# Two head pairs per attention step with merged products, and the rounded parts of q and k and the sums' 1e-9 on GpSimd

## The chip, the cores and the metric

The kernel runs on one core of one Trainium2 chip. The metric is the device time of one execution in microseconds (us); lower is better. The engines are named as in the profile: PE is TensorE's products, PEld its loads of fixed operands, DVE is VectorE, ACT is ScalarE, POOL is GpSimd, SP is SyncE, which issues most DMAs.

## The reference

```python
def _attn_ref(q, k, v, n_global, n_local):        # 4 batches, 8 heads, 768 tokens, 64 wide
    scores = scale * np.matmul(q, k.transpose(0, 1, 3, 2)) + bias     # a slope per head times the distance
    scores = np.where(is_global | is_local, scores, -1000000000.0)     # 8 first keys, 96 last keys
    a = np.exp(scores - np.max(scores, axis=-1, keepdims=True))
    a = a / (np.sum(a, axis=-1, keepdims=True) + 1e-09)
    return np.matmul(a, v)

def reference(...):
    x = attention, its heads side by side           # [3072, 512]
    x = _moe_ref(x, w_gate, w1, w2)                 # each token to the best of 8 experts, 512 -> 1024 -> 512, times its gate
    return _moe2_ref(x, w_in, w_out, a, b)          # rational feed-forward, 512 -> 2048 -> 512
```

## The kernel before, in words

Attention comes first and takes the first quarter of the time. It has 24 units (u: a batch and a tile of 128 queries), each of four head pairs (hp). Since only 96 local and 8 global keys count, a unit's window is 232 keys wide (WIN), or 128 for a tile that starts a sequence. A loop over t (L746 on) goes through the 96 steps (u, hp). Everything is emitted in the order of that loop, and each engine works through its own instructions in that order. A step t has five groups of products on PE, each for another pair:

- stD (L644) of step t-5: the attended values, transposed back and multiplied with the gate's weights, into ps_ox (L647); DVE scales them into x (L653) and lw (L657)
- stA (L575) of step t: the scores, 6 products on half the rows, `sj` (L586), as a rounded part and a rest of q and k (qh, ql and two parts in kr)
- stC (L630) of step t-3: the probabilities times v, into ps_o (L638), copied to oT by ACT (L641)
- stB (L608) of step t-1: 4 transposes of probabilities into pt (L616), copied to pT (L624; of one pair in four on ACT, L622)
- emit_tstep (L503): 2 of the 4 transposes of the next tile of q or k, ps_qk (L512).

After each second half of a tstep ACT copies ps_qk to `raw` and rounds that to qh or a part of kr (L524), and POOL subtracts the two for the rest (L525). Between A and B, stA2 (L589) has DVE add the mask and find the extreme of a row (`nn`, `mn`, L600) and ACT take the exponential with the sum `sm` (`pp`, L604). In stB DVE adds 1e-9 to the sums (L619) and inverts them (L626).

Between such instructions `fill()` emits one small step of routing each, mostly on DVE: which expert a token goes to, its gate, its sorted position `pos` (L215), and then scatters on POOL (`scatter`, L136, tid) and a table (L198). Tokens are routed in groups of 4, 7, 6, 3, 3 and 1 units. Once the fourth group is routed, the first tokens of expert 0 are fetched early: their numbers are read back (L128, eidx) behind all scatters, their rows gathered (L250, raw), and, in the string TAILS that emits what follows the loop, scaled on DVE (letter G, `scale_x`, L254) and transposed (X), and the expert is begun (E). TAILS also drains the last steps (B, C, D with the distance from the end), and F is a fill. POOL also splits the first expert's weights during attention (wa_l, L315). Scores have three PSUM banks (psS), pt two, ps_qk, ps_o and ps_ox one each.

Of the kernel before, what the change touches and what calls it, by code (L numbers as in the profile page):

```python
# [20 lines left out]
P = 128  # L21
# [12 lines left out]
TAILS = "D5 G F1 C3 C2 B1 X0 C1 F3 D4 X1 D3 F3 F7 F1 E2 D2 F2 F1 E2 F2 F2 F1 F3 E1 F5 D1"  # L34
# [5 lines left out]
WARM2 = 2, 2, 2, 4  # L40
LOADS = ("k0", "ll", "lg", "q0", "k1", "q1")
POOLQ = ""
MS = (7, 2, 4, 2)
# [5 lines left out]
def kernel(  # L49
# [206 lines left out]
    def put_xT(xh, xl, x, t, r, ps=None):  # L256
        """Puts a token tile of r rows, transposed, in columns t*P on of both parts."""
# [13 lines left out]
    def early_steps(w, x, h, banks, ends=(0, FC1 + KC)):  # L271
        """The early tile's products in small steps, each followed by what it leaves to do for other engines."""
# [44 lines left out]
    def expert_chunks(wh, wl, e1, e2):  # L317
        """Split steps of an expert's weights; e1: [DM, F1] and e2: [F1, DM] sources."""
# [10 lines left out]
    # ================= attention, window of the fast path =================  # L329
    with first as sx:  # L330
# [8 lines left out]
        # the inputs' rings lie where the first expert's operands will  # L339
# [61 lines left out]
        # masks: distance times slope, plus NEG where nothing is kept; the first for the tiles that start a  # L401
        # sequence, the second for the others, whose window is the local tail, the global keys and the tile
# [33 lines left out]
        # constants that are not needed at once  # L436
# [40 lines left out]
        # q and k transposed, [d of two heads, pair, token], in two float32r parts. The keys of a sequence lie  # L477
        # side by side, each tile behind a copy of the global keys, so that a window is one stretch of columns.
# [6 lines left out]
        def emit_first(nm, part):  # L485
            """A half of the first tile's heads, without detours."""
# [16 lines left out]
        def emit_tstep(step, part):  # L503
# [9 lines left out]
            if part == 1:  # L513
# [10 lines left out]
                nc.scalar.activation(qh, raw, AF.Copy)  # L524
# [19 lines left out]
        seq = [(u, hp) for u in range(units) for hp in range(NP)]  # L544
# [12 lines left out]
        # the second mask's own tile is the first mask, but for the columns of the global keys  # L557
# [4 lines left out]
        def fill(pe=False):  # L562
            """One small step of the routing, between two large ones; those with products only where pe."""
# [11 lines left out]
        def stA(u, hp):  # L575
            bb, i = divmod(u, NI)
            w = P if i == 0 else WIN
            s2 = []
            k1 = (i + 1) * GK
            for j in range(2):  # L580
                sj = psS.tile([P, 512], F32, name="sj")
                s2.append(sj)
            for n, (x, y) in enumerate(((0, 0), (0, 1), (1, 0))):
                for j in range(2):
                    hd = slice(j * D, (j + 1) * D)
                    nc.tensor.matmul(s2[j][:, 0:w], qT[u][x][hd, hp, :], kr[hd, y, hp, k1 - w:k1], start=n == 0, stop=n == 2)  # L586
            st[u, hp] = s2

        def stA2(u, hp):  # L589
            i = u % NI  # L590
            w = P if i == 0 else WIN
            s2 = st[u, hp]
            sm = wk.tile([P, 2], F32, name="sm", bufs=5)
            pr = []
            for j in range(2):
                h = 2 * hp + j
                nn = wk.tile([P, WIN], F32, name=f"nn{j}")
                mn = wk.tile([P, 1], F32, name=f"mn{j}")
                bmh = bm[:, h, WIN:WB] if i == 0 else bm[:, h, 0:WIN]
                nc.vector.tensor_tensor_reduce(nn[:, 0:w], s2[j][:, 0:w], bmh, op0=ALU.add, op1=ALU.min,  # L600
                                               scale=1.0, scalar=3.0e38, accum_out=mn)
                fill()
                pp = wk.tile([P, WIN], F32, name=f"pp{j}")
                nc.scalar.activation(pp[:, 0:w], nn[:, 0:w], AF.Exp, scale=-1.0, bias=mn, accum_out=sm[:, j:j + 1])  # L604
                pr.append(pp)
            st[u, hp] = [pr, sm]

        def stB(u, hp):  # L608
            i = u % NI
            w2 = P // 2 if i == 0 else HWIN  # L610
            pr, sm = st[u, hp]
            pt = psT.tile([P, 2, 2, P], F32, name="pt")
            for j in range(2):
                pv = pr[j][:, 0:2 * w2].rearrange("p (c r) -> p r c", r=2)
                for r in range(2):
                    nc.tensor.transpose(pt[0:w2, j, r, :], pv[:, r, :], ident)  # L616
            pT = wk.tile([HWIN, 2, 2, P], F32, name="pT", bufs=3)
            rs = wk.tile([P, 2], F32, name="rs", bufs=7)
            nc.vector.tensor_scalar(rs, sm, 1e-9, None, op0=ALU.add)  # L619
            fill()  # L620
            if hp in ONACT:
                nc.scalar.activation(pT[0:w2], pt[0:w2], AF.Copy)  # L622
            else:
                nc.vector.tensor_copy(pT[0:w2], pt[0:w2])  # L624
            fill()
            nc.vector.reciprocal(rs, rs)  # L626
            fill()
            st[u, hp] = [pT, rs]

        def stC(u, hp):  # L630
            i = u % NI
            w2 = P // 2 if i == 0 else HWIN
            pT, rs = st[u, hp]
            vt = vts[u]
            ox = psM.tile([P, 512], F32, name="ps_o")
            for r in range(2):
                for j in range(2):
                    nc.tensor.matmul(ox[j * D:(j + 1) * D, 0:P], vt[0:w2, 2 * hp + j, r, :], pT[0:w2, j, r, :],  # L638
                                     start=(r == 0), stop=(r == 1))
            oT = wk.tile([P, P], F32, name="oT", bufs=4)  # L640
            nc.scalar.activation(oT, ox[:, 0:P], AF.Copy)  # L641
            st[u, hp] = [oT, rs]

        def stD(u, hp):  # L644
            oT, rs = st.pop((u, hp))
            ox = psM.tile([P, 512], F32, name="ps_ox")
            nc.tensor.matmul(ox[:, 0:P + 2 * E], oT, iw[:, hp, :], start=True, stop=True)  # L647
            if hp == 0:
# [4 lines left out]
            nc.vector.tensor_tensor(x[:, hp * P:(hp + 1) * P].rearrange("p (j d) -> p j d", j=2),  # L653
                                    ox[:, 0:P].rearrange("p (j d) -> p j d", j=2),
                                    rs.unsqueeze(2).to_broadcast([P, 2, D]), op=ALU.mult)
            fill()
            nc.vector.tensor_tensor(lw[:, 2 * hp:2 * hp + 2, :],  # L657
                                    ox[:, P:P + 2 * E].rearrange("p (j e) -> p j e", j=2),
                                    rs.unsqueeze(2).to_broadcast([P, 2, E]), op=ALU.mult)
            if hp == NP - 1:  # L660
# [15 lines left out]
        # the first tokens of expert 0, from when all but the last groups are routed; done again below if too few  # L676
# [21 lines left out]
        def e_step(n, lag=1):  # L698
            """n small steps of the early tile; what they leave to other engines comes some steps later."""
# [46 lines left out]
        for t in range(L):  # L746
            if t < L:
                u, hp = seq[t]
                bb, i = divmod(u, NI)
                if 0 < t < 3:  # L750
                    emit_tstep(*nxt.pop(0))
                if t == NP + 2:
                    filler.append(look)
                if hp == (u == 0):
                    if u + 2 < units:
                        load_v(u + 2)
                    for lb, li in loads.get(u, []):
                        load_qk(lb, li)
                if hp == 0 and u >= 5 and u % 2 == 1 and wst:
                    dh, dl, src, n = wst.pop(0)  # L760
                    wld.append((dh, dl, load_w(src, n)))
                if hp == 0 and 2 <= u < 2 + sum(groups[-2:]):
                    r0 = (units - sum(groups[-2:]) + u - 2) * P
                    nc.sync.dma_start(xs[r0:r0 + P, :], zrow)
# [903 lines left out]
```

## Time and profile before

| what | value |
|---|---|
| time, median of 3 runs | 1171.92 us (1169.7 to 1175.31) |
| span of the profiled execution | 1169.0 us |
| PE busy | 1109.0 us (95%) |
| DVE, ACT, POOL busy | 954.6 us (82%), 760.1 us (65%), 434.6 us (37%) |

The span is that of one execution under the profiler, from first to last instruction; it is 2.9 us below the median of the runs and inside their spread to 0.7 us. Start times below are microseconds from the start of the span. The page's shares are means over stages with different limits; attention is the stretch from about 9 to 275 us.

### The profile page before, as it was taken

The page shows a single profiled execution, that of the slowest core. Times are in us where ns is not written, and L with a number is a line of the kernel's source. Part 1 is how long each engine was busy: PE and PEld are TensorE (multiplying, and loading weights), DVE is VectorE, ACT ScalarE, POOL GpSimd, SP SyncE. Part 2 cuts the span into 40 slices and gives each one's busy share as a digit, 9 for nine tenths or more (in the row PEclk, how much of TensorE's full clock was granted, in tenths as well). Part 3 has the DMA queues.
Part 4 walks back from the last instruction along what each step waited for, and adds up shares of the span by engine and source line. Part 5 has one row for each costly group of instructions (what it writes and reads, how often), then busy time and mean ns, then how long its engine had stood idle before and what let it go on. Part 6 is the DMA issues. An engine that isn't in the chain of part 4 may idle for free.

```text
span 1169.0 us, 19466 instructions
## 1 busy us (share of the span) xinstructions
PE 1109.0 (95%) x6636; PEld 982.8 (84%) x6636; DVE 954.6 (82%) x2200; ACT 760.1 (65%) x1695; POOL 434.6 (37%) x454
## 2 busy tenths in 40 slices
PE   8998988987699999999997999999999999999997
PEld 7876776766699888999996888999999999999996
DVE  7897878774667967887667999989898998989985
ACT  5886777662254555554555777777777777777774
POOL 4253444532422323132114535344342535344342
PEclk9998989798799999999999999999999999999999
DMA  9887787403477877887663000000100000000000
GB/s 177 186 132 162 164 94 173 87 20 105 114 226 251 302 243 248 283 302 269 211 204 123 1 27 28 28 28 1 46 10 28 28 27 28 19 27 10 1 28 27
DMA packets 122820, 130.65 MB, mean 112 GB/s; under 512 B 62799, under 2 KB 92671, under 8 KB 122704
## 3 DMA queue, kind: packets, MB, share of 16 engines
q1 hardware_dynamic: 108416, 99.78, 32.7%
q0 software_dynamic: 8624, 22.48, 5.6%
q10 hardware_dynamic: 5664, 6.98, 1.6%
q8 instruction: 56, 0.92, 0.4%
q14 instruction: 60, 0.49, 0.2%
HBM read 99.60 MB, written 29.61 MB: 111 GB/s over the span
## 4 chain that ended last, share of the span: by engine, by line
PE 59%; DVE 7%; ACT 2%; issue 2%; DMA 2%; POOL 1%; ACTq 0%; POOLq 0%; DVEq 0%; SPq 0%
PE acc L268 10%; PE acc L267 10%; PE acc L269 10%; PE ph L267 7%; PE ph L268 7%; PE ph L269 7%; PE ps_t L267 3%; PE ps_t L269 3%; PE ps_t L268 3%; DVE ta L1546 1%; DVE tcc L1545 1%; DVE ta L1595 1%; PE ps_t L260 1%; DVE tcc L1605 1%; DMA ysT<-y 1%
## 5 line engine op out<-in xcount | busy, mean ns | idle before, releaser
L1560 POOL TENSOR_TENSOR gl<-tcc,gh 128x384 fp32r<-128x384 f32 x127 | 128.9, 1015 | 293.8 <-ACT gh L1554 229.1
L267 PE MATMUL acc<-wa_h,gh 128*128 128x512 f32 x384 | 150.2, 391 | 5.9 <-ACT gh L1554 4.3
L269 PE MATMUL acc<-wa_h,gl 128*128 128x512 f32 x384 | 151.4, 394 | 1.7 <-POOL gl L1560 1.7
L268 PE MATMUL acc<-wa_l,gh 128*128 128x512 f32 x384 | 151.3, 394 | 0.0
L1545 DVE SCALAR_TENSOR_TENSOR tcc<-tcc,cf,tb 128x384 f32<-128x384 f32 x128 | 117.9, 921 | 13.7 <-DVE tcc L1605 0.5
L1596 ACT ACTIVATE tb<-ta,cf 128x384 f32<-128x384 f32 x128 | 79.0, 617 | 42.8 <-DVE ta L1595 32.8
L1595 DVE SCALAR_TENSOR_TENSOR ta<-ta,cf,tb 128x384 f32<-128x384 f32 x128 | 81.4, 636 | 31.0 <-ACT tb L1590 29.7
L604 ACT ACTIVATE pp<-nn,mn 128x232 f32<-128x232 f32 (+1 forms) x192 | 88.8, 465 | 26.6 <-DVE mn L600 23.5
L1546 DVE SCALAR_TENSOR_TENSOR ta<-ta,cf,tb 128x384 f32<-128x384 f32 x128 | 103.3, 807 | 0.0
L269 PEld LDWEIGHTS acc<-wa_h,gl 128*128 128x128 f32 x384 | 72.1, 188 | 20.0 <-POOL gl L1560 4.7
L267 PE MATMUL ph<-xh,wb_h 128*128 128x384 f32 (+3 forms) x252 | 86.8, 344 | 1.7 <-DVE tcc L1605 1.2
L267 PEld LDWEIGHTS acc<-wa_h,gh 128*128 128x128 f32 x384 | 72.1, 188 | 19.0 <-ACT gh L1554 5.7
L268 PE MATMUL ph<-xl,wb_h 128*128 128x384 f32 (+3 forms) x252 | 86.3, 343 | 0.3 <-DVE xl L953 0.2
L269 PE MATMUL ph<-xh,wb_l 128*128 128x384 f32 (+3 forms) x252 | 86.1, 342 | 0.0
L268 PEld LDWEIGHTS acc<-wa_l,gh 128*128 128x128 f32 x384 | 72.0, 188 | 11.4
L616 PE MATMUL pt<-ident,pp 128*116 128x128 f32 (+1 forms) x384 | 71.6, 311 | 2.3 <-ACT pp L604 2.3
L1589 ACT ACTIVATE ta<-ph 128x384 f32<-128x384 f32 x78 | 38.1, 488 | 54.0 <-PE ph L269 54.0
L600 DVE CUSTOM_DVE_ANT_0 nn<-sj,bm 128x232 f32<-128x232 f32 (+1 forms) x192 | 65.8, 373 | 6.8 <-PE sj L586 4.7
L1551 DVE SCALAR_TENSOR_TENSOR tcc<-ta,tcc 128x384 f32<-128x384 f32 x128 | 70.4, 550 | 0.0
L616 PEld LDWEIGHTS pt<-ident,pp 128*116 128x116 f32 (+1 forms) x384 | 49.3, 185 | 20.9 <-issue 15.3
L1554 ACT ACTIVATE gh<-tcc 128x384 fp32r<-128x384 f32 x128 | 65.1, 509 | 2.3 <-DVE tcc L1551 2.3
L1601 ACT ACTIVATE tb<-tb 128x384 f32<-128x384 f32 x128 | 65.1, 509 | 0.0
(335 smaller groups left out, 3352.9 us busy)
## 6 DMA issues: line engine op xcount, KB each, us to landing
wst<-in_moe_w_dram SPq DMA_DIRECT2D x72, 512.0 KB
wst<-in_moe_w_in_dram SPq DMA_DIRECT2D x16, 512.0 KB
wst<-in_moe_w_out_dram SPq DMA_DIRECT2D x16, 512.0 KB
xs<-x SPq DMA_DIRECT2D x24, 256.0 KB
hh<-in_v_dram SPq DMA_DIRECT2D x17, 256.0 KB
wf_in<-cv POOLq DMA_DIRECT2D x16, 256.0 KB
wf_out<-cv POOLq DMA_DIRECT2D x16, 256.0 KB
wst<-wf_in SPq DMA_DIRECT2D x8, 512.0 KB
```

The source lines that it names most:

```text
L267: nc.tensor.matmul(ps, lh, rh, start=first, stop=False)
L268: nc.tensor.matmul(ps, lh, rl, start=False, stop=False)
L269: nc.tensor.matmul(ps, ll, rh, start=False, stop=last)
L600: nc.vector.tensor_tensor_reduce(nn[:, 0:w], s2[j][:, 0:w], bmh, op0=ALU.add, op1=ALU.min, scale=1.0, scalar=3.0e38, accum_out=mn)
L604: nc.scalar.activation(pp[:, 0:w], nn[:, 0:w], AF.Exp, scale=-1.0, bias=mn, accum_out=sm[:, j:j + 1])
L616: nc.tensor.transpose(pt[0:w2, j, r, :], pv[:, r, :], ident)
L1545: nc.vector.scalar_tensor_tensor(pc_, pc_, na0, pb_, op0=ALU.add, op1=ALU.mult)
L1546: nc.vector.scalar_tensor_tensor(pa_, pa_, one, pb_, op0=ALU.add, op1=ALU.mult)
L1551: nc.vector.scalar_tensor_tensor(pc_, pa_, -2.0, pc_, op0=ALU.add, op1=ALU.mult)
L1560: eng.tensor_tensor(gl, prev[2], gh.bitcast(F32), op=ALU.subtract)
L1595: nc.vector.scalar_tensor_tensor(ta, ta, b1, tb, op0=ALU.mult, op1=ALU.add)
L1596: nc.scalar.activation(tb, ta, AF.Ln, bias=one)
```

## The change

Attention's loop now takes two head pairs (HG = 2) at a time: 48 steps (u, hg), here called double steps. Each of the five groups on PE holds the products of both pairs, one behind the other: 12 for the scores in two banks (a pair at columns 0 and 256 of each), 8 for ps_o, 2 for ps_ox, 8 transposes of probabilities, and two tsteps. The copy to oT, x and lw take both pairs in one instruction. The lags are 1, 2 and 3 double steps in place of 1, 3 and 5 steps. The rounding at L524 is on GpSimd, ahead of the subtraction there, and so is the addition of 1e-9 (now L617, four columns at once); the inversion stays on DVE and stands in stC, behind the copy to oT (L651). A double step has 11 fills where two steps had 14. The lists of warm-up products and TAILS have new numbers. The diff, without the hunks that only take comments away:

```diff
-TAILS = "D5 G F1 C3 C2 B1 X0 C1 F3 D4 X1 D3 F3 F7 F1 E2 D2 F2 F1 E2 F2 F2 F1 F3 E1 F5 D1"
+TAILS = "D3 G F1 C2 B1 X0 C1 F3 D2 X1 F3 F7 F1 E2 D1 F2 F1 E2 F2 F2 F1 F3 E1 F5"
-WARM2 = 2, 2, 2, 4
+WARM2 = 4, 6
-MS = (7, 2, 4, 2)
+MS = (7, 2, 4, 4)
...
-                nc.scalar.activation(qh, raw, AF.Copy)
+                nc.gpsimd.tensor_copy(qh, raw)
                 (nc.vector if u < SUBV else nc.gpsimd).tensor_tensor(ql, raw, qh.bitcast(F32), op=ALU.subtract)
...
+        HG = 2
+        NG2 = NP // HG
+        seq = [(u, hg) for u in range(units) for hg in range(NG2)]
...
+        def stA(u, hg):
+            s2 = [psS.tile([P, 512], F32, name="sj") for j in range(2)]
+            for a in range(HG):
+                hp = HG * hg + a
+                for n, (x, y) in enumerate(((0, 0), (0, 1), (1, 0))):
+                    for j in range(2):
+                        hd = slice(j * D, (j + 1) * D)
+                        nc.tensor.matmul(s2[j][:, a * 256:a * 256 + w], qT[u][x][hd, hp, :], kr[hd, y, hp, k1 - w:k1],
+                                         start=n == 0, stop=n == 2)
...
+        def stB(u, hg):
+            rs = wk.tile([P, HG, 2], F32, name="rs", bufs=5)
+            nc.gpsimd.tensor_scalar(rs, sm, 1e-9, None, op0=ALU.add)
+            pts = []
+            for a in range(HG):
+                pt = psT.tile([P, 2, 2, P], F32, name="pt")
...
+            for a in range(HG):
+                pT = wk.tile([HWIN, 2, 2, P], F32, name="pT", bufs=3)
+                fill()
+                if HG * hg + a in ONACT:
+                    nc.scalar.activation(pT[0:w2], pts[a][0:w2], AF.Copy)
+                else:
+                    nc.vector.tensor_copy(pT[0:w2], pts[a][0:w2])
...
+        def stC(u, hg):
+            for a in range(HG):
+                for r in range(2):
+                    for j in range(2):
+                        nc.tensor.matmul(ox[j * D:(j + 1) * D, a * P:(a + 1) * P], vt[0:w2, 2 * (HG * hg + a) + j, r, :],
+                                         pTs[a][0:w2, j, r, :], start=(r == 0), stop=(r == 1))
+            oT = wk.tile([P, HG, P], F32, name="oT", bufs=2)
+            nc.scalar.activation(oT, ox[:, 0:HG * P].rearrange("p (a q) -> p a q", a=HG), AF.Copy)
+            nc.vector.reciprocal(rs, rs)
...
+            if t >= 3:
+                stD(*seq[t - 3])
+            stA(u, hg)
+            if t >= 2:
+                stC(*seq[t - 2])
+            stA2(u, hg)
...
+            if t >= 1:
+                stB(*seq[t - 1])
+            for _ in range(3 if t == 0 else 2):
+                if nxt:
+                    emit_tstep(*nxt.pop(0))
...
             fill(True)
+            fill(True)
```

First, PE's stream in the loop, one whole step of before and the start of the next (ps_ox is the output of D, sj the scores of A, ps_o that of C, pt of B, ps_qk of the transposes):

```order
L647 MATMUL ps_ox<-iw,oT 128x144
L586 MATMUL sj<-kr,qh 128x232 x4
L586 MATMUL sj<-kr,ql 128x232 x2
L638 MATMUL ps_o<-pT,hl 64x128 x4
L616 MATMUL pt<-ident,pp_1990 116x128 x2
L616 MATMUL pt<-ident,pp_1995 116x128 x2
L512 MATMUL ps_qk<-ident,xh 128x128 x2
L647 MATMUL ps_ox<-iw,oT 128x144
```

And one whole double step of the changed kernel:

```order
L659 MATMUL ps_ox<-iw,oT 128x144 x2
L588 MATMUL sj<-kr,qh 128x232 x4
L588 MATMUL sj<-kr,ql 128x232 x2
L588 MATMUL sj<-kr,qh 128x232 x4
L588 MATMUL sj<-kr,ql 128x232 x2
L647 MATMUL ps_o<-pT,hh 64x128 x8
L624 MATMUL pt<-ident,pp_1917 116x128 x2
L624 MATMUL pt<-ident,pp_1927 116x128 x2
L624 MATMUL pt<-ident,pp_1922 116x128 x2
L624 MATMUL pt<-ident,pp_1932 116x128 x2
L512 MATMUL ps_qk<-ident,xl 128x128 x4
```

The same products now stand in half as many groups, five per two pairs in place of ten.

Second, POOL's stream at a place in the middle of the loop, before, where a weight split (wa_l) stands between subtractions:

```order
L525 TENSOR_TENSOR kr<-raw,kr 128x4x128
L315 TENSOR_TENSOR wa_l<-wst,wa_h 128x1024
L525 TENSOR_TENSOR ql<-raw,qh 128x512
L525 TENSOR_TENSOR kr<-raw,kr 128x4x128
L525 TENSOR_TENSOR ql<-raw,qh 128x512
```

And a like place of the changed kernel:

```order
L315 TENSOR_TENSOR wa_l<-wst,wa_h 128x1024
L617 TENSOR_SCALAR rs<-sm 128x4
L524 CAST kr<-raw 128x4x128
L525 TENSOR_TENSOR kr<-raw,kr 128x4x128
L617 TENSOR_SCALAR rs<-sm 128x4
L524 CAST qh<-raw 128x512
L525 TENSOR_TENSOR ql<-raw,qh 128x512
```

A cast stands ahead of each subtraction, and the sums' addition (rs), which DVE's inversion reads, is queued behind subtractions and weight splits.

Third, DVE's stream at the end of attention, from the fourth group's positions (pos, L215) to the scaling of the early gathered rows (raw, L254), which stands in TAILS. Before, there are eight steps of pairs between the two (each with an x at L653); the two ends:

```order
L215 TENSOR_TENSOR pos<-em_4509,rank 128x3
L527 CAST kr<-kr 128x8x8
L653 TENSOR_TENSOR x<-ps_ox,rs 128x128
L657 TENSOR_TENSOR lw<-ps_ox,rs 128x16
...
L657 TENSOR_TENSOR lw<-ps_ox,rs 128x16
L666 TENSOR_REDUCE lg<-lw 128x8
L254 TENSOR_SCALAR raw<-raw 128x512 x2
L163 TENSOR_REDUCE mx<-lg 128x3
```

Of the changed kernel:

```order
L215 TENSOR_TENSOR pos<-em_4144,rank 128x3
L633 COPY pT<-pt 116x512 x2
...
L667 TENSOR_TENSOR x<-ps_ox,rs 128x256
L671 TENSOR_TENSOR lw<-ps_ox,rs 128x32
L651 RECIPROCAL rs<-rs 128x4
...
L633 COPY pT<-pt 116x512
L667 TENSOR_TENSOR x<-ps_ox,rs 128x256
L671 TENSOR_TENSOR lw<-ps_ox,rs 128x32
L680 TENSOR_REDUCE lg<-lw 128x8
L254 TENSOR_SCALAR raw<-raw 128x512 x2
```

Only two double steps' x stand between them now; `pos` falls into the double step t = 46, and L254 follows D of t = 45 right after the loop's end.

## Rows read from the trace of the kernel before

**Rows 1.** The page's first line.
```profile
span 1169.0 us, 19466 instructions
```
**Rows 2.** Windows: start:end, us, busy of each engine, PEclk, DMA share, GB/s.
```profile
20.00:265.00 245.00, 224.81 (x2019) 176.08 (x2016) 200.57 (x937) 178.45 (x583) 101.48 (x98) 0.92 0.67 129
200.00:222.00 22.00, 20.67 (x130) 15.79 (x128) 15.19 (x71) 11.62 (x39) 9.19 (x11) 0.61 0.47 106
```
**Rows 3.** Timeline of PE, one step: start us, duration us, instruction.
```profile
123.49 0.49 PE L586 MATMUL sj<-kr,qh 64*128 64x232 f32 x4
...
124.02 0.66 PE L638 MATMUL ps_o<-pT,hh 116*64 116x128 f32 x8
124.61 0.70 PE L616 MATMUL pt<-ident,pp 128*116 128x128 f32 x4
125.15 0.38 PE L512 MATMUL ps_qk<-ident,hl 128*128 128x128 f32 x2
...
125.71 0.38 PE L586 MATMUL sj<-kr,qh 64*128 64x232 f32 x2
```
**Rows 4.** Timeline of PE, one step between 200 and 222 us.
```profile
211.61 0.77 PE L586 MATMUL sj<-kr,qh 64*128 64x232 f32 x4
...
212.53 1.12 PE L638 MATMUL ps_o<-pT,hh 64*64 64x128 f32 x8
213.57 1.12 PE L616 MATMUL pt<-ident,pp 128*116 128x128 f32 x4
214.49 0.63 PE L512 MATMUL ps_qk<-ident,hl 128*128 128x128 f32 x2
...
215.53 0.56 PE L586 MATMUL sj<-kr,qh 64*128 64x232 f32 x2
```
**Rows 5.** Timeline of PE: first scores of steps t = 4 and t = 92.
```profile
20.27 0.37 PE L586 MATMUL sj<-kr,qh 64*128 64x232 f32 x2
254.12 0.37 PE L586 MATMUL sj<-kr,qh 64*128 64x232 f32 x2
```
**Rows 6.** Waits of PE and of DVE, 20 to 265 us: total, times, longest.
```profile
PE ps_ox L647 <- DVE lw L657: 13.8, 11, 3.4
DVE x L653 <- DMA xs<-x: 9.5, 3, 3.7
```
**Rows 7.** Groups by line, 0 to 400 us: busy us, mean ns | idle before, releasers.
```profile
L619 DVE TENSOR_SCALAR rs<-sm 128x2 f32<-128x2 f32 x96 | 45.9, 478 | 0.0
L524 ACT ACTIVATE qh<-raw 128x512 fp32r<-128x512 f32 x23 | 14.5, 632 | 0.7
L525 POOL TENSOR_TENSOR ql<-raw,qh 128x512 fp32r<-128x512 f32 x23 | 29.6, 1285 | 54.1 <-issue 26.8 <-ACT qh L524 23.0 <-DVE rs L619 4.1
```
**Rows 8.** Timeline of POOL and DVE at 132 us.
```profile
132.42 2.35 POOL L315 TENSOR_TENSOR wa_l<-wst,wa_h 128x1024 fp32r<-128x1024 f32 x1 [1.76 <-ACT wa_h L314]
132.50 2.29 DVE L184 TENSOR_TENSOR cum<-cum,oh 128x8 bf16<-128x8 bf16 x1
```
**Rows 9.** Groups by form, other one-input work of POOL, 0 to 320 us.
```profile
L443 POOL COPY iw<-ident 128x128 f32<-128x128 f32 x4 | 1.0, 285 | 0.0
L396 POOL MEMSET iw<- 128x576 f32 x1 | 0.6, 572 | 0.0
```
**Rows 10.** Timeline of POOL: the last subtraction ahead of a new unit.
```profile
125.42 1.30 POOL L525 TENSOR_TENSOR ql<-raw,qh 128x512 fp32r<-128x512 f32 x1 [3.63 <-issue]
```
**Rows 11.** Timeline, early fetch: positions, last scatter, first gather, scaling.
```profile
245.19 0.14 DVE L215 TENSOR_TENSOR pos<-em,rank 128x3 int32<-128x3 f32 x1
250.42 0.96 POOL L136 DMA_INDIRECT tid<-tok,pos  x1 [0.22 <-issue]
262.48 0.98 POOL L250 DMA_INDIRECT raw<-xs,eidx  x1 [9.68 <-issue]
266.99 0.48 DVE L254 TENSOR_SCALAR raw<-raw 128x512 f32<-128x512 f32 x1
```
**Rows 12.** Waits of SP, 245 to 265 us.
```profile
SPq L128 <- DMA tid<-tok,pos: 10.2, 1, 10.2
```

More of the change, by code (lines that the diff above doesn't have):

```diff
@@ L590, in stA2 @@
+            st[u, hg] = s2
+        def stA2(u, hg):
             i = u % NI
             w = P if i == 0 else WIN
-            s2 = st[u, hp]
-            sm = wk.tile([P, 2], F32, name="sm", bufs=5)
-            pr = []
+            s2 = st[u, hg]
+            sm = wk.tile([P, HG, 2], F32, name="sm", bufs=4)
+            pr = {}
             for j in range(2):
[L596 to L605, printed above, removed]
@@ L606, in stA2 @@
-            st[u, hp] = [pr, sm]
-        def stB(u, hp):
+                for a in range(HG):
+                    h = 2 * (HG * hg + a) + j
+                    nn = wk.tile([P, WIN], F32, name="nn", bufs=4)
+                    mn = wk.tile([P, 1], F32, name="mn", bufs=6)
+                    bmh = bm[:, h, WIN:WB] if i == 0 else bm[:, h, 0:WIN]
+                    nc.vector.tensor_tensor_reduce(nn[:, 0:w], s2[j][:, a * 256:a * 256 + w], bmh, op0=ALU.add,
+                                                   op1=ALU.min, scale=1.0, scalar=3.0e38, accum_out=mn)
+                    fill()
+                    pp = wk.tile([P, WIN], F32, name=f"pp{a}{j}", bufs=2)
+                    nc.scalar.activation(pp[:, 0:w], nn[:, 0:w], AF.Exp, scale=-1.0, bias=mn, accum_out=sm[:, a, j:j + 1])
+                    pr[a, j] = pp
@@ L609, in stB @@
+            st[u, hg] = [pr, sm]
+        def stB(u, hg):
             i = u % NI
             w2 = P // 2 if i == 0 else HWIN
[L611 to L630, printed above, removed]
+            pr, sm = st[u, hg]
+            rs = wk.tile([P, HG, 2], F32, name="rs", bufs=5)
@@ L631, in stC @@
+            st[u, hg] = [pTs, rs]
+        def stC(u, hg):
             i = u % NI
             w2 = P // 2 if i == 0 else HWIN
-            pT, rs = st[u, hp]
+            pTs, rs = st[u, hg]
             vt = vts[u]
             ox = psM.tile([P, 512], F32, name="ps_o")
[L636 to L645, printed above, removed]
+            for a in range(HG):
+                for r in range(2):
+                    for j in range(2):
+                        nc.tensor.matmul(ox[j * D:(j + 1) * D, a * P:(a + 1) * P], vt[0:w2, 2 * (HG * hg + a) + j, r, :],
+                                         pTs[a][0:w2, j, r, :], start=(r == 0), stop=(r == 1))
@@ L646, in stD @@
+            oT = wk.tile([P, HG, P], F32, name="oT", bufs=2)
+            nc.scalar.activation(oT, ox[:, 0:HG * P].rearrange("p (a q) -> p a q", a=HG), AF.Copy)
+            nc.vector.reciprocal(rs, rs)
+            st[u, hg] = [oT, rs]
+        def stD(u, hg):
+            oT, rs = st.pop((u, hg))
             ox = psM.tile([P, 512], F32, name="ps_ox")
-            nc.tensor.matmul(ox[:, 0:P + 2 * E], oT, iw[:, hp, :], start=True, stop=True)
-            if hp == 0:
+            OW = P + 2 * E
+            for a in range(HG):
+                nc.tensor.matmul(ox[:, a * OW:(a + 1) * OW], oT[:, a, :], iw[:, HG * hg + a, :], start=True, stop=True)
+            if hg == 0:
@@ L746 @@
         for t in range(L):
[L747 to L764, printed above, removed]
-                if hp == 1 and u >= 5 and u % 2 == 0 and wld:
-                    split_w(*wld.pop(0), nc.gpsimd)
-            if 0 <= t - 5 < L:
-                stD(*seq[t - 5])
+            u, hg = seq[t]
+            bb, i = divmod(u, NI)
+            if t == 1:
+                emit_tstep(*nxt.pop(0))
+            if t == 3:
+                filler.append(look)
+            if hg == (u == 0):
+                if u + 2 < units:
+                    load_v(u + 2)
+                for lb, li in loads.get(u, []):
+                    load_qk(lb, li)
+            if hg == 0 and u >= 5 and u % 2 == 1 and wst:
+                dh, dl, src, n = wst.pop(0)
+                wld.append((dh, dl, load_w(src, n)))
+            if hg == 0 and 2 <= u < 2 + sum(groups[-2:]):
+                r0 = (units - sum(groups[-2:]) + u - 2) * P
+                nc.sync.dma_start(xs[r0:r0 + P, :], zrow)
+            if hg == 1 and u >= 5 and u % 2 == 0 and wld:
+                split_w(*wld.pop(0), nc.gpsimd)
+            if t >= 3:
+                stD(*seq[t - 3])
             if t < len(WARM2):
                 keep_warm(psM, "ps_ox", WARM2[t])
-            if t < L:
-                stA(*seq[t])
-            if 0 <= t - 3 < L:
-                stC(*seq[t - 3])
-            while t == NP and filler:
+            stA(u, hg)
+            if t >= 2:
+                stC(*seq[t - 2])
+            while t == NG2 and filler:
                 fill()
-            if t < L:
-                stA2(*seq[t])
+            stA2(u, hg)
             if t == 0:
```

45 lines of the change are left out of this document (20 added, 25 removed).

## The prediction

> **What bounds the kernel now.** The profiled execution spans 1169.0 us [rows 1]; the median of the runs shown is 2.9 us above that, so I sum on the span and add 2.9 at the end. The change touches only attention, so the first thing to read is the table of windows over 20 to 265 us, the steady part of the loop [rows 2]. PE is busy 224.81 of 245 us, DVE 200.57, ACT 178.45, POOL 101.48: PE sets the pace, but it stands idle 20.2 us, and its granted clock is 0.92 in the mean, down to 0.61 in 200 to 222 us.
>
> Next I read PE's timeline at two steps, one at full clock (2.4 GHz) and one at half (1.2 GHz). By starts, the groups A, C, B and T with D take 0.53, 0.59, 0.54 and 0.56 us, a step of 2.22 us [rows 3]; at the lower clock 0.92, 1.04, 0.92 and 1.04, a step of 3.92 [rows 4]. A pure count of cycles would double. What doesn't is a part that the clock doesn't touch: twice the first less the second, 0.14, 0.14, 0.16 and 0.08, together 0.52 us a step. I read it as the cost of passing from one group to the next.
>
> Then the loop as a whole: the scores of step 4 start at 20.27 and those of step 92 at 254.12 [rows 5], 88 steps in 233.85 us. At 2.22 that would be 195.4, so 38.5 us are lost, to idle PE and to steps at the lower clock. The waits say where the idle comes from [rows 6]: 13.8 us at D for DVE's lw, since ps_ox has one bank, and behind that DVE's x waiting for a DMA that still reads the x buffer (9.5 us in three waits). Another part is DVE held by POOL: a routing addition on 8 columns took 2.29 us because it started with POOL's weight split and ended with it [rows 8], and the addition of 1e-9 to two columns averages 478 ns [rows 7], far more than so little data needs.
>
> **The change part by part.** *Merged groups.* The same products stand in half as many groups, so a double step saves one step's fixed part: 2 x 2.22 - 0.52 = 3.92 us at full clock. From step 4 to step 92 lie 44 double steps, which save 44 x 0.52 = 22.9 us. That is the gain at the upper end; if the fixed part belongs to each product's first use rather than to a change of group, the saving can go down to none. I take the whole, since the part is alike (0.14 to 0.16) in A, C and B, which differ in their number of products.
>
> The Trainium skill, TensorEngine Tiling (Array Packing), Key Properties, says that a change of tiling mode, not just of tile, drains TensorE. A, C and B each begin with another form of tile, and there the rows have 0.44 of the 0.52 us; by the rule alone the saving is 44 x 0.44 = 19.4 us, 3.5 less than by the rows.
>
> *The 1e-9 on GpSimd.* DVE loses 45.9 us in 96 instructions [rows 7], 0.96 a double step. DVE's load is 200.57 / 46 = 4.36 a double step and falls to 3.4, below the new 3.92. POOL gains one addition on four columns, which no row shows: from about 0.1 to the 0.48 that DVE's took; I take 0.2. The inversion on DVE now waits for POOL, where this addition is queued behind the cast, the subtraction and, in eight double steps, a weight split of 2.35 us [rows 8]. Behind the inversion stand the next scores' nn and the pT copy, and PE waits for those. The rs of a double step is needed one double step later, so about 2 us are in hand by my estimate, and only the eight splits can overrun them: nothing to 12 us. I put it at the same size as the stalls that leave DVE with the old addition, so nothing net.
>
> *The cast on GpSimd.* ACT sheds 0.63 us a double step [rows 7], from 178.45 / 46 = 3.88 to 3.25, and gains nothing that shows, since it wasn't the bound. POOL's cast of 512 columns isn't in the trace. From below, a memset of 576 columns took 0.572, so 0.51 for 512; a copy of 128 columns took 0.285 [rows 9]; from above, the subtraction, with two inputs, takes 1.285 [rows 7]. I take 0.75, between the two one-input rows carried to 512 columns (0.51 and 1.14), because part of the copy's 0.285 is a fixed start. POOL's load becomes 101.48 / 46 = 2.21, plus 0.75, plus 0.2: 3.16 a double step, at the upper ends 3.97. It is hidden as long as it stays under 3.92.
>
> The path that could show is that of q: transposes, raw, rounding, subtraction, next unit's scores. Before, the last subtraction ends at 125.42 + 1.30 = 126.72 [rows 10], and the scores that need it start a step after 125.71 [rows 3], at 127.93: 1.21 us in hand. The distance in PE's order is two steps before and one double step after, nearly alike; the four transposes in one group start the copy some 0.2 later, and the cast is 0.12 longer than ACT's rounding. 0.9 are left, at the upper end of the cast 0.35. So nothing on the path.
>
> *Buffers and DMA.* x is written again after three double steps, 11.8 us, in place of five steps, 11.1, so the three waits for the DMA [rows 6] stay about as they are. The loads of the stretch, 129 GB/s, would be 142 if it shrinks by 22 us. I let all 38.5 us of lost time stand: the loads, splits and routing that cause it are still there, and what DVE gains in one place it waits for in another.
>
> *Loop.* Scores of double step 46 then start at 20.27 + 0.5 (a longer fill of the pipeline, estimated) + 44 x 3.92 + 38.5 = 231.8, where the same pair was at 254.12: 22.3 us earlier.
>
> *What comes late next.* Not all of that survives. Before, the fourth group's positions are done at 245.19, eight steps before the loop's end; three scatters follow, the last at 250.42; the rows are gathered from 262.48 on, and the scaling in the tail starts at 266.99 [rows 11]. SP waits 10.2 us of that for the scatters to land [rows 12]. These 21.8 us are mostly DMA latency and don't shrink with a faster loop. After, positions stand in double step 46, and the scaling, L254, right behind the loop. DVE works in order: it would be at L254 some 9 us after the scores of double step 46, and finds no rows there. Positions come about 2.8 us behind these scores (four nn at some 0.5 with what stands between), at 234.6. The chain then takes 20.8, since three scatters of 0.96 need some 4.2 of the 5.2 us that they had. So the scaling starts at 255.4 in place of 266.99: 11.6 us earlier, and not 22. Meanwhile DVE stands for about 14 us at L254, with pT copies and inversions behind it that PE waits for. From the scaling on, the work is the same as before, in the same order, so what is left of the gain goes through to the end: 1169.0 - 11.6 + 2.9 = **1160.3**.
>
> **The rivals.**
>
> *Lost time shrinks too (faster still).* The addition of 1e-9 that cost DVE 45.9 us is gone, and D's bank is released by one lw instead of two. If of the 38.5 us a third goes, 13 us, the scaling is at 242 and the time 1147. For it: the 13.8 us that PE waits for lw are DVE's lateness. Against it: 9.5 us of DVE's lateness are a DMA's, and routing stays stuck behind POOL.
>
> *The fixed part isn't the group's (no change).* If merging saves half of the 0.52, 11.4 us are missing and 1171.7 comes out, since the early fetch takes the rest. For it: within a merged A, loads of fixed operands change as often as before, and PEld is busy 176 of 245 us [rows 2]. Against it: only the small T and D group, without a new form of tile, has the small part.
>
> *GpSimd becomes the limit (slower).* With the cast at 1.285 and the addition at 0.48, POOL has 3.97 us of work in a double step of 3.92, before any scatter or split comes on top; the inversion waits on POOL every time, and so do the next unit's scores. From a mean double step of 3.92 + 11.6 / 44 = 4.18 on, the change gains nothing. At 4.35 the loop is 18.9 us longer than forecast: 1179.2. For it: POOL and DVE hold each other up, as the 2.29 us show [rows 8], and POOL is to work 1.4 times as long. Against it: in the trace POOL sat idle before the subtractions of q alone for 54.1 us [rows 7].
>
> The Trainium skill, GPSIMD Engine Reference, Specifications, speaks for this one: it says that GpSimd shares its SBUF interfaces with VectorE and gets in the way of instructions with two SBUF inputs. The stuck addition above, with two inputs, agrees; the cast lengthens the time in which this can happen.
>
> **How the numbers follow.** Forecast 0.45, with a range of its own of 1154 to 1167 (the chain of the fetch 2 us shorter, the skipped 0.08 or the rs waits against me); less lost time 0.17; no change 0.18; GpSimd 0.20. About 0.5% (5.9 us) is what a measurement of this kernel can tell from no change, so faster means under 1166. Faster: 0.41 of the forecast's 0.45 and 0.17, 0.58; within: 0.04 and most of the third case, 0.21; slower: the fourth and a little of the third, 0.21. The range reaches from 1145, with a third of the losses gone, to 1177, most of the way to GpSimd's case.
>
> **What would show it.** On PE's timeline at full clock a double step takes 3.9 us, with starts of A, C and B some 0.15 closer than two single ones. L524 on POOL takes 0.7 to 0.8. The busy time of L619 on DVE is gone, and DVE's wait for POOL at L651 is short. L254 has a wait of 10 us or more for the gathered rows, and PE a gap there. I am wrong if PE's merged groups last twice the single ones; if PE waits at L588 for POOL; if DVE waits for rs in every double step; or if the fetch comes early enough, and L254 doesn't wait.

## The result, and the profile after

The changed kernel takes 1163.74 us in the median of four runs (1160.89 to 1165.41), the kernel before 1172.26 beside it. The ratio is 0.99, with a 95% interval of 0.9867 to 0.9933; in a second series on another chip (y1 below) it is 0.9929 (0.9894 to 0.9964). The forecast was 1160, in a range of 1145 to 1177, and the direction is right too. The way there is not: two large errors of the prediction have opposite signs. One execution of y4 and one of z1 below ran at a mean granted clock of 0.75 and 0.74, took 1323.94 and 1352.96 us, and are left out of the medians and ratios given.

First the page's first line and the windows table of the changed kernel, over the same stretch as [rows 2] and over the loop alone.

```profile
span 1163.7 us, 19354 instructions
```
```profile
20.00:265.00 245.00, 202.18 (x2089) 173.96 (x2085) 174.02 (x754) 147.83 (x502) 147.41 (x199) 0.92 0.71 141
20.00:216.00 196.00, 177.01 (x1881) 152.87 (x1878) 152.38 (x648) 135.63 (x460) 132.21 (x173) 0.97 0.84 160
```

In the loop PE is idle 19 us, as before (20.2; over the same 44 double steps it is 20.3 and was 18.1), but its granted clock is 0.97 instead of 0.92. Beyond 216 us attention runs out, and the other 24 us of idle PE in the first line lie there. PE's timeline shows why the loop is shorter: the first line is the scores of double step 2, then comes one whole double step at full clock, and the last line is the scores of double step 46.

```profile
17.10 0.37 PE L588 MATMUL sj<-kr,qh 64*128 64x232 f32 x1
...
35.50 0.48 PE L588 MATMUL sj<-kr,qh 64*128 64x232 f32 x4
...
36.36 1.09 PE L647 MATMUL ps_o<-pT,hh 116*64 116x128 f32 x16
37.39 1.14 PE L624 MATMUL pt<-ident,pp 128*116 128x128 f32 x8
38.36 0.60 PE L512 MATMUL ps_qk<-ident,hl 128*128 128x128 f32 x4
38.80 0.66 PE L659 MATMUL ps_ox<-iw,oT 128*128 128x144 f32 x4
39.38 0.49 PE L588 MATMUL sj<-kr,qh 64*128 64x232 f32 x4
...
220.11 0.37 PE L588 MATMUL sj<-kr,qh 64*128 64x232 f32 x1
```

A double step takes 39.38 - 35.50 = 3.88 us, where two single steps took 4.44 [rows 3]. By starts, it is 0.20 us shorter in the scores, 0.15 in ps_o, 0.11 in the transposes of probabilities and 0.10 from T to the next scores. The scores of double step 46 start at 220.11, those of the same pair before at 254.12 [rows 5]: 34 us earlier.

The groups by line (0 to 300 us) give what no row of before had, the cast and the addition on GpSimd.

```profile
L525 POOL TENSOR_TENSOR ql<-raw,qh 128x512 fp32r<-128x512 f32 x23 | 29.8, 1294 | 2.0
L524 POOL CAST qh<-raw 128x512 fp32r<-128x512 f32 x23 | 14.2, 619 | 16.7 <-PE sj L588 8.6 <-ACT raw L520 8.0
L617 POOL TENSOR_SCALAR rs<-sm 128x4 f32<-128x4 f32 x48 | 10.7, 223 | 4.0
```

And DVE's waits, 20 to 265 us:

```profile
DVE raw L254 <- DMA raw<-xs,eidx: 16.9, 2, 16.5
DVE x L667 <- DMA xs<-x: 13.5, 3, 8.4
DVE rs L651 <- POOL rs L617: 8.9, 8, 2.4
```

DVE stands 16.5 us at the scaling of the early rows, and its waits for the sums are 8.9 us in eight pieces. PE's waits for GpSimd at the scores, 20 to 240 us, which the prediction put at nothing:

```profile
PE sj L588 <- POOL ql L525: 2.5, 5, 0.9
PE sj L588 <- POOL qh L524: 0.7, 2, 0.3
```

So 34 us were gained by the end of the loop, and 5.3 us are left at the end of the span. The timeline of the changed kernel from there on (DVE and PE) says where they went:

```profile
223.55 0.15 DVE L215 TENSOR_TENSOR pos<-em,rank 128x3 int32<-128x3 f32 x1
...
244.99 0.49 DVE L254 TENSOR_SCALAR raw<-raw 128x512 f32<-128x512 f32 x1 [16.52 <-DMA raw<-xs,eidx]
...
267.65 0.19 PE L1250 MATMUL ps_t<-cums,ones 128*128 128x8 bf16 x1 [8.62 <-DVEq L835]
...
281.99 2.69 DVE L1306 CAST fi<-sidx 128x24 f32<-128x24 int32 x1 [7.42 <-DMA sidx<-tid]
...
292.00 0.58 PE L267 MATMUL ph<-xh,wa_h 128*128 128x256 f32 x1 [15.59 <-DVE hl L294]
...
310.67 0.48 PE L267 MATMUL ph<-wa_h,cv 128*128 128x512 f32 x1 [2.49 <-PEq L1428]
```

The third line is the counts of tokens per expert, the fourth a read-back that the plan (the order and places of the experts' work, which DVE computes from the counts) waits for, the last one the first of the large products, with which PE's long stretch of work begins. The counts and the first large product in the timeline of before:

```profile
288.93 0.17 PE L1237 MATMUL ps_t<-cums,ones 128*128 128x8 bf16 x1 [6.83 <-DVEq L822]
...
317.86 0.47 PE L267 MATMUL ph<-wa_h,cv 128*128 128x512 f32 x1 [2.10 <-ACT nop L1445]
```

The gain over before is 34.0 us at the scores of the last unit, 22.0 at the scaling (266.99 [rows 11]), 21.3 at the counts, and 7.2 at the large products. The first loss, 12 us, is the one predicted: the early fetch doesn't shrink. The second, 14 us, wasn't: from the counts to the large products the kernel before takes 28.9 us, the changed one 43.0, and 15.6 of these are PE's wait for hl at 292.00. What waits there are products of the early tile. Counted by form, ahead of the counts, before and then after:

```profile
L267 PE MATMUL sj<-xh,wa_h x24: 276/282/387, 271.4 to 281.6; 128*128 128x256 f32 x24
```
```profile
L267 PE MATMUL sj<-xh,wa_h x8: 280/390/588, 252.1 to 258.5; 128*128 128x256 f32 x8
```

Each of these is one of three products of a step, so 24 of the early tile's steps stand ahead of the counts before, and 8 after. The other 16 come behind the counts, where their hl (DVE) is queued behind the plan, which itself waits 7.4 us for a read-back. The reason is in the first line of the diff: TAILS ended with D1, so the last group's routing steps were all left for the closing loop, which emits one early step behind each. In the new TAILS 16 fills follow D1. They use these routing steps up, and the early steps that would have gone with them come only after the counts.

### The profile page after: what moved, and what is told of

It is laid out like the page before. It is cut to its first block, busy times and chain, and to the rows that moved or that the text cites. A ratio compares the mean times of both kernels' runs of the same rounds, so it can differ in the third digit from the quotient of the medians.

```text
span 1163.7 us, 19354 instructions
## 1 busy us (share of the span) xinstructions
PE 1076.6 (93%) x6636; PEld 972.3 (84%) x6636; DVE 915.1 (79%) x1960; ACT 725.0 (62%) x1601; POOL 476.7 (41%) x548
## 4 chain that ended last, share of the span: by engine, by line
PE 63%; DVE 6%; issue 1%; DMA 1%; ACT 1%; POOL 0%; POOLq 0%; ACTq 0%; DVEq 0%
PE acc L268 10%; PE acc L267 10%; PE acc L269 10%; PE ph L267 8%; PE ph L268 8%; PE ph L269 8%; PE ps_t L269 3%; PE ps_t L267 3%; PE ps_t L268 3%; DVE ta L1559 1%; DVE tcc L1558 1%; DVE ta L1608 1%; PE ps_t L260 1%; DVE tcc L1618 1%; DVE tcc L1613 1%
## 5 line engine op out<-in xcount | busy, mean ns | idle before, releaser
L267 PE MATMUL ph<-xh,wa_h 128*128 128x464 f32 (+3 forms) x152 | 53.7, 353 | 16.3 <-DVE hl L294 15.6
L1085 DVE TENSOR_TENSOR wa_l<-wst,wa_h 128x1024 fp32r<-128x1024 f32 x31 | 40.0, 1292 | 20.9 <-ACT wa_h L1084 20.7
```

The costliest lines, as they stand in the source:

```text
L267: nc.tensor.matmul(ps, lh, rh, start=first, stop=False)
```

## The experiments

Theory: the loop gains because merged groups save changes of tile form on PE, not because DVE and ACT are relieved; the gain is given back in the tail, first to the early fetch and then to the early steps that moved behind the counts. Rivals: the relief of DVE and ACT is what helps; and the plan's own DMA chain, not the early steps, sets the start of the large products. The series x, y and z ran on three chips, each with the kernel before beside it (1168.17, 1168.06 and 1167.52 us), so runs of different series are compared by their ratios to it.

**x1_early16**: the early steps put back, nothing else.

```diff
-TAILS = "D3 G F1 ... F1 F3 E1 F5"
+TAILS = "D3 G F1 ... F1 F3 E1 F5 E16"
```

> The changed kernel with 16 more steps of the early tile at the end of the tail string, nothing else. Theory (the gain of the loop is given back because 16 of the early tile's steps moved behind the counts, where they wait for the plan on VectorE): the wait of 15.6 us for hl before the first large products shrinks below 8, these products start at 296 to 304 instead of 310.7, and the time falls to 1150 to 1158. Rival (the plan's own chain, the read-back of the sorted tokens and the loads behind it, sets the start of the large products): they start at 309 or later and the time stays at 1161 to 1166.

Measured: 1149.70 us, ratio to before 0.9826 (0.9772 to 0.9879). The counts, the large products, and the early steps ahead of the counts:

```profile
268.52 0.17 PE L1250 MATMUL ps_t<-cums,ones 128*128 128x8 bf16 x1 [7.25 <-PEq L835]
...
294.46 0.47 PE L267 MATMUL ph<-wa_h,cv 128*128 128x512 f32 x1 [2.13 <-ACT nop L1458]
```
```profile
L267 PE MATMUL sj<-xh,wa_h x24: 278/281/384, 249.8 to 260.8; 128*128 128x256 f32 x24
```

From the counts to the large products it is 25.9 us in place of 43.0, and the counts are only 0.9 us later, since the 16 steps fit into time in which PE waited. The wait for hl is gone. The rival falls: the plan and its read-back are as they were, and the large products start 16 us earlier. Their start and the time both lie a little below what was expected (296 and 1150).

**x2_merge_only** and **x3_pool_only**: each half of the change alone.

```diff
 x2, on the changed kernel
-                nc.gpsimd.tensor_copy(qh, raw)
+                nc.scalar.activation(qh, raw, AF.Copy)
...
-            nc.gpsimd.tensor_scalar(rs, sm, 1e-9, None, op0=ALU.add)
+            nc.vector.tensor_scalar(rs, sm, 1e-9, None, op0=ALU.add)
```
```diff
 x3, on the kernel before
-                nc.scalar.activation(qh, raw, AF.Copy)
+                nc.gpsimd.tensor_copy(qh, raw)
...
-            nc.vector.tensor_scalar(rs, sm, 1e-9, None, op0=ALU.add)
+            nc.gpsimd.tensor_scalar(rs, sm, 1e-9, None, op0=ALU.add)
...
-            nc.vector.reciprocal(rs, rs)
-            fill()
...
             nc.scalar.activation(oT, ox[:, 0:P], AF.Copy)
+            nc.vector.reciprocal(rs, rs)
```

> The changed kernel with the rounding back on ScalarE and the 1e-9 back on VectorE; merged groups, lags and tail stay. Theory (merging carries the loop): double steps of 3.9 us at full clock, scores of double step 46 within 5 us of 220, time 1160 to 1168. Rival (the relief of VectorE and ScalarE carries it): scores of double step 46 ten us or more later, time 1170 or above.

> The kernel before, one pair a step, with only the rounding and the 1e-9 on GpSimd and the inversion behind the copy to oT. Theory (merging carries the loop): steps stay 2.2 us at full clock, scores of step 92 start 0 to 7 us before 254, time 1167 to 1174. Rival (the relief carries it): step 92 starts 15 us or more earlier, time 1162 or below.

Measured: merging alone 1158.10 us, ratio 0.9896 (0.9849 to 0.9943), which is the whole change's; the scores of double step 46 start at 211.95, 8 us before those of the changed kernel and further than the 5 us expected, and the time is below the 1160 expected. The 8 us are not more than profiles differ: the same loop starts these scores at 217.65 and 221.44 in y4 and z3, the changed one at 215.16 in y1. The moves alone 1177.45 us, ratio 1.006 (1.0023 to 1.0098), slower than before and above the 1174 expected. There the full-clock step stays at 2.2 us, the scores of step 92 start at 256.32, 2 us later than before where 0 to 7 earlier was expected, and then the tail loses more. GpSimd and DVE of x3_pool_only, timeline:

```profile
254.77 1.29 POOL L525 TENSOR_TENSOR ql<-raw,qh 128x512 fp32r<-128x512 f32 x1
264.31 1.04 POOL L250 DMA_INDIRECT raw<-xs,eidx  x1 [8.26 <-issue]
265.66 0.97 POOL L250 DMA_INDIRECT raw<-xs,eidx  x1 [0.30 <-issue]
266.70 0.80 POOL L619 TENSOR_SCALAR rs<-sm 128x2 f32<-128x2 f32 x3
```
```profile
266.94 0.17 DVE L641 RECIPROCAL rs<-rs 128x2 f32<-128x2 f32 x1 [9.49 <-POOL rs L619]
```

The addition is queued behind the early gathers, which wait for the tokens' numbers, and so the inversion on DVE waits 9.5 us with the pairs behind it. That is the price of the move that this trace shows.

**y1_changed_again, y2_sums_on_vector, y3_round_on_scalar**: the changed kernel on another chip, and beside it with one of the two moves taken back (y2 by the second hunk of x2's diff, y3 by the first).

> The changed kernel as it is, to stand beside the next ones on one chip. Ratio to the kernel before 0.985 to 0.994.

> The changed kernel with the sums' 1e-9 back on VectorE, the rounding still on GpSimd. Theory (queued behind casts, subtractions and splits on GpSimd, the addition holds VectorE's inversion, 8.9 us in the trace of the changed kernel): that wait is gone and the time is 3 to 8 us below the changed kernel's. Rival (VectorE pays as much again when it does the addition itself and stands behind GpSimd): within 2 us of the changed kernel.

> The changed kernel with the rounding back on ScalarE, the 1e-9 still on GpSimd. Theory (the cast of 0.61 us is hidden): within 3 us of the changed kernel, the waits of TensorE's scores for ql and qh (4.4 us in all with their loads) gone or small. Rival (the cast makes GpSimd's queue late, and with it the sums): 4 us or more below the changed kernel, and VectorE's wait for the sums at the inversion falls below 3 us.

Measured: 1159.68 us, 0.9929 (0.9894 to 0.9964); 1162.95, 0.9951 (0.9922 to 0.9979); 1159.80, 0.9917 (0.9886 to 0.9948). The intervals overlap: no change of the time by either move is shown. For the sums the theory missed: there is no gain of 3 to 8 us in taking them back, the median is 3.3 us higher, a little beyond the rival's 2. On DVE the addition averages 483 ns again:

```profile
L617 DVE TENSOR_SCALAR rs<-sm 128x4 f32<-128x4 f32 x48 | 23.2, 483 | 0.0
```

For the rounding, DVE's wait for the sums does fall, as the rival said (y1, then y3, 20 to 240 us), but not the time:

```profile
DVE rs L651 <- POOL rs L617: 6.5, 7, 1.9
```
```profile
DVE rs L651 <- POOL rs L617: 1.2, 2, 0.8
```

PE's waits at the scores for ql and qh are gone in y3, as the theory said.

y1's profile is a second one of the changed kernel, and its tail repeats the first: scores of double step 46, counts and large products on PE.

```profile
215.16 0.91 PE L588 MATMUL sj<-kr,qh 64*128 64x232 f32 x4
...
262.18 0.19 PE L1250 MATMUL ps_t<-cums,ones 128*128 128x8 bf16 x1 [8.65 <-DVEq L835]
...
304.44 0.47 PE L267 MATMUL ph<-wa_h,cv 128*128 128x512 f32 x1 [2.13 <-ACT nop L1458]
```

The gain over before is 39.0 us at these scores, 27.3 at the scaling (239.69), 26.8 at the counts, 13.4 at the large products and 13.3 at the end of the span (1155.7). The two losses are there again, 12 and 13 us, and behind the large products nothing is lost.

**x4_scale_late, y4_merge_late, z3_merge_late2**: the tail put in another order, to take the scaling's wait out of the last pairs' way; x4 with the changed loop, y4 and z3 with x2's.

```diff
 x4 and y4
-TAILS = "D3 G F1 C2 B1 X0 C1 F3 D2 X1 F3 F7 F1 E2 D1 F2 F1 E2 F2 F2 F1 F3 E1 F5"
+TAILS = "D3 F1 C2 B1 C1 F3 D2 F3 F7 D1 F1 G F3 X0 X1 F2 E2 F1 E2 F2 F2 F1 E1 F5 E16"
 z3
+TAILS = "D3 F1 C2 B1 C1 F3 D2 F3 F9 D1 F20 G X0 X1 E21"
```

> As x1_early16, but with the scaling of the early rows and their transposes behind the last attention pairs and the last groups' routing begun ahead of it. Theory (the 16.5 us that VectorE stands at the scaling hold back the last tokens' routing, so the counts): the counts come 10 us or more before 267, time 5 to 15 us below x1_early16. Rival (the routing of the last groups is held elsewhere, by GpSimd's queue behind the gathers or by the early tile): counts within 4 us of x1_early16's, time within 4 us of it.

> x2_merge_only with the tail of x4_scale_late: merged groups alone, nothing moved to GpSimd, scaling late, 16 more early steps. Theory (in x4_scale_late the last inversion waits 8.8 us for a sum that is queued behind the gathers on GpSimd): that wait is gone, the last two positions come by 232 and 243 instead of 239.8 and 250.8, the counts 6 to 12 us earlier than 263, and the time 4 to 12 us below x4_scale_late's. Rival (the scatters and gathers themselves, not the sums, set the start of the large products): counts earlier, but the large products within 3 us of 288.5 and the time within 3 us of x4_scale_late's.

> y4_merge_late with all of the last group's routing ahead of the scaling, then transposes and 21 early steps at a stretch. If the routing's place behind the scaling holds the counts, they come 4 to 10 us before 262.6 and the time falls to 1132 to 1138. If the early tile's own products, which stand ahead of the counts on TensorE, hold them, counts and time stay within 3 us of y4_merge_late.

Measured: x4 1144.47 us, ratio 0.9784 (0.9733 to 0.9835); y4 1140.02, 0.975 (0.9678 to 0.9821); z3 1139.48, 0.9738 (0.9661 to 0.9815). All three are the best measured, but they aren't told apart, and x4's interval overlaps x1's. x4's counts come at 263.2, 5 us ahead of x1's and not 10. DVE of x4, timeline:

```profile
237.99 0.18 DVE L651 RECIPROCAL rs<-rs 128x4 f32<-128x4 f32 x1 [8.84 <-POOL rs L617]
```

With the scaling out of the way, the last inversion waits behind the same gathers as in x3. y4 has no such wait, and its last but one positions do come 5 us sooner (234.68 for 239.78), but the last ones not (250.88 for 250.83), nor the counts (262.6). Its large products start where x4's do, which was the rival's forecast (x4, then y4):

```profile
288.47 0.47 PE L267 MATMUL ph<-wa_h,cv 128*128 128x512 f32 x1 [2.08 <-ACT nop L1458]
```
```profile
287.76 0.47 PE L267 MATMUL ph<-wa_h,cv 128*128 128x512 f32 x1 [2.27 <-ACT nop L1458]
```

In z3 all routing is ahead of the scaling, and it gains nothing more: the last positions are there at 241.9, the counts only at 267.4, behind the early tile and a last wait of PE of 5.2 us. What is left there looks like the early tile's own chain, rows, scaling, transposes and 24 steps; no run takes that apart.

**z1_split_scores** and **z2_split_transposes**: the price of a change of group, on the changed kernel.

```diff
 z1
-            stA(u, hg)
-            if t >= 2:
-                stC(*seq[t - 2])
+            for part in range(2):
+                stA(u, hg, part)
+                if t >= 2:
+                    stC(*seq[t - 2], part)
 z2: stB calls tsteps() between the transposes of its two pairs
-            if t >= 1:
-                stB(*seq[t - 1])
...
+            if t >= 1:
+                stB(*seq[t - 1], tsteps)
```

> The changed kernel with scores and ps_o taken pair by pair again inside a double step: scores of the first pair, ps_o of its first pair, then the second of each; two more changes of tile form. Theory (the saved part is what TensorE pays on each change from one form of group to another, 0.14 us at scores and 0.14 at ps_o by the steps before): double steps at full clock of 4.12 to 4.22 instead of 3.885, time 6 to 16 us above the changed kernel, ratio to the kernel before about 1.00. Rival (fewer starts of instructions or the longer lead of other engines saves it): double steps stay at 3.88 to 3.95.

> The changed kernel with the transposes of q and k between the two pairs' transposes of probabilities: one more group, but all of the same tile form. Theory in its form by tile (only a change of form costs): double steps at full clock stay within 0.02 of 3.885 and the time within 3 us. Theory in its form by group (every new group costs): 0.04 to 0.16 more a double step, 2 to 7 us.

Measured: z1 1169.20 us, ratio 1.0003 (0.997 to 1.0037): with two changes of form put back in a double step, no gain of the time is left. In z1's profile the scores of double step 46 still start 27 us before those of the kernel before (226.67); the tail, with the two losses of the changed kernel, takes that. PE's timeline of z1:

```profile
29.04 0.49 PE L588 MATMUL sj<-kr,qh 64*128 64x232 f32 x4
...
29.57 0.66 PE L649 MATMUL ps_o<-pT,hh 116*64 116x128 f32 x8
30.16 0.49 PE L588 MATMUL sj<-kr,qh 64*128 64x232 f32 x4
...
30.68 0.66 PE L649 MATMUL ps_o<-pT,hh 116*64 116x128 f32 x8
31.27 1.14 PE L624 MATMUL pt<-ident,pp 128*116 128x128 f32 x8
...
33.27 0.38 PE L588 MATMUL sj<-kr,qh 64*128 64x232 f32 x2
```

A double step takes 4.23 us, 0.35 more than merged and a little above the 4.22 expected, so 0.17 a change. z2 1163.12 us, ratio 0.9961 (0.9923 to 0.9998); PE's timeline of it, one double step:

```profile
33.15 0.49 PE L588 MATMUL sj<-kr,qh 64*128 64x232 f32 x4
...
35.03 0.70 PE L624 MATMUL pt<-ident,pp 128*116 128x128 f32 x4
35.57 0.60 PE L512 MATMUL ps_qk<-ident,hl 128*128 128x128 f32 x4
36.01 0.60 PE L624 MATMUL pt<-ident,pp 128*116 128x128 f32 x4
36.45 0.66 PE L661 MATMUL ps_ox<-iw,oT 128*128 128x144 f32 x4
37.03 0.48 PE L588 MATMUL sj<-kr,qh 64*128 64x232 f32 x4
```

It takes 3.88, as merged, with one group more but none of another form. Every second double step took 4.05: there ps_o waited for ACT's copy of pT (0.9 us in four waits from 30 to 60 us), which now stands behind the copy of ps_qk. So half of the full-clock steps kept to the 0.02 expected, and the others are late by that wait. The time doesn't decide: by the ratios it is 4 to 7 us above the changed kernel's, outside the 3 expected of a cost by form, but the intervals overlap, and the waits for pT lengthen it too. The steps do: what costs is the change of form, not the group.

## Why the prediction was right or wrong

- *Merged groups.* Right. 3.92 was forecast, 3.88 came; 44 double steps save 24.6 us at full clock. x2 and x3 show that the merged loop brings the gain and not the two moves, and z1 that the changes of form are what the step saves. The whole 0.52 a step is saved (0.56 came), but it isn't the group's cost, as the prediction read it: it belongs to the three changes of tile form in a step (scores, ps_o, probabilities), 0.17 to 0.19 us each. By starts, 0.10 of it lies between T and the next scores, groups that begin without a new form, so z1 and z2 place the cost and not the starts. The Trainium skill, TensorEngine Tiling (Array Packing), Key Properties, says that a change of tiling mode, not just of tile, drains TensorE. z1 and z2 agree with it, at 0.17 us for a change put back and 3.88 us with one more group of the same form; the runs show the time, not that it is a drain. The rival that half of the saving is lost falls.
- *The 1e-9 and the cast on GpSimd.* Right that they bring nothing net, and nearly right in price: the cast 0.62 us for 0.75, the addition 0.22 for 0.2. DVE's waits for the sums, 8.9 us in eight, lie in the nothing to 12 us that the prediction gave. GpSimd's rival falls, as 3.88 us a double step shows. The path of q was put at nothing; it cost PE 3.2 us in seven waits, a small piece of that rival and one of the prediction's own signs of being wrong, and y3, without it, is no faster. x3 shows the wait that I had missed: the addition queued behind gathers.
- *Lost time.* The term of 38.5 us was too large. From 17.10 to 220.11 are 203.0 us; 44 double steps of 3.88 are 170.7; lost are 32.3. The same count gives 27 to 32 us in the four profiles with the changed loop (this one, y1, x1, x4), 24 to 32 in the three without the two moves (x2, y4, z3), and 40.3 in x3, with one pair a step. So the rival of shrinking losses was half right, and not by DVE's relief. In the changed kernel's profile PE's idle time stayed, and the DMA waits grew (13.5 us for 9.5), but more of the loop was at the higher clock, 0.97 for 0.92; z3 lost 32.4 at 0.92, so the clock alone doesn't explain it, and the cause stays open.
- *Start of the loop.* 0.5 us late was forecast; the first steady scores came at 17.10, 3.2 us early. No run tried why. So of the 34.0 us at the last unit's scores 24.6 are the shorter step, 6.2 less lost time and 3.2 the start, and the cause of the first alone is shown.
- *The early fetch.* Right in size: positions to scaling 21.4 us for 20.8, DVE's stop 16.5 for 14. With the earlier loop the scaling came at 245.0, 10.4 us ahead of the forecast 255.4.
- *"From the scaling on, the work is the same as before, in the same order."* This step failed. The order was in front of me in TAILS: D1 moved ahead of 16 fills. It cost 14 us in the trace; x1, which puts the 16 steps back, is 9 to 12 us faster by the ratios (1149.70 us). Only because the loop's error, 10.4 us at the scaling, lay on the other side did 1160 come out near 1163.74: that the number is so close is luck.
- Of the 7.2 us at the large products 5.3 are left at the end of the profiled span. In y1's profile nothing is lost there (13.4 and 13.3), so these 1.9 are no more than two profiles differ by.

## What to carry to other kernels

A gain in a loop reaches the end only through what follows: write down the gain at three or four milestones of both traces (loop, hand-over, first work of the next stage), and look for the first one where it shrinks. Where a string or a list interleaves two streams, count for each milestone how many steps of the other stream stand ahead of it in the new order; here 16 steps behind a wait took 14 of the 21 us that had come as far as the counts. And give an engine's queue no small operation that a busy engine needs if the same queue holds a DMA that waits for another DMA: x3 and x4 show waits of 9.5 and 8.8 us, though y4, without that wait, is not measurably faster.

## What the runs showed of the hardware

- A change of tile form on TensorE (half rows, half columns, full) costs 0.17 to 0.19 us at full clock: 46 x 2 of them took the ratio to the kernel before from 0.99 and 0.9929 to 1.0003. Going from one group to another of full form cost nothing that shows (3.88 with and without).
- An addition of 1e-9 to four columns took 223 ns on GpSimd and 483 on average on VectorE, whose mean for two columns was as long [rows 7]. But that mean isn't the addition's own length. In the kernel before, 69 of the 96 took 0.29 us or less; each of the other 27 took 0.67 us or more and ended within 0.04 us of the end of an instruction of GpSimd, as here (timeline of before). So most of what the move takes off VectorE is waiting for GpSimd.

```profile
86.32 1.27 POOL L525 TENSOR_TENSOR kr<-raw,kr 128x512 fp32r<-128x512 f32 x1 [2.55 <-ACT kr L524]
...
86.48 1.14 DVE L619 TENSOR_SCALAR rs<-sm 128x2 f32<-128x2 f32 x1
```

- A cast of 512 columns took 619 ns on GpSimd, as long as ScalarE's 632 [rows 7].
- GpSimd's work grew by 46 us from 20 to 265 (147.41 for 101.48) without a longer full-clock step on TensorE; TensorE's waits for it at the scores came to 3.2 us.
